# First block of a hedgehog attention kernel: x and the values' weights fetched first, a constant turned on TensorE until x is there, one tile's values and then the queries' folding in written order

## The chip, the cores and the metric

The kernel runs on one core of one Trainium2 chip. A core has five engines that run side by side, each taking its own instructions in order: TensorE (matrix products, PE in the profile), VectorE (DVE), ScalarE (ACT), GpSimd (POOL) and SyncE (SP), which here only issues DMA transfers. The metric is the device time of one execution in microseconds (us); the time of a kernel is the median over its runs.

## The reference

Two layers share their weights. Each layer adds an attention and a dense part to x, and each part reads x normalized over its 640 columns.

```python
qkv = (layernorm(x) @ wqkv)            # (2048, 640) @ (640, 1920): 32 heads of 20
pq = einsum("bhsd,hdf->bhsf", q, w_phi)   # a 20 x 20 matrix for each head; the same for k
phi_q = concat([softmax(pq), softmax(-pq)])           # 40 features a head; the same for k
kv, z = einsum(phi_k, v), sum(phi_k over s)
o = (phi_q @ kv) / (phi_q @ z + 1e-6)
x = x + o @ wo
x = x + mish(layernorm(x) @ w1 + b1) @ w2             # 640 -> 1536 -> 640
```

x is 2048 x 640, all in float32.

## The kernel before

**Tiles.** The 2048 rows are worked in 8 blocks of 256 rows, each of two tiles of 128. A block of x is normalized and then *turned*: TensorE transposes the rows in 128 x 128 pieces (ten for a block, `Transposed.step`, L280), so that the 640 columns lie on the partitions. Each float32 operand is split into a high part that TensorE takes at its faster type (made on ScalarE, tile names ending in `h`) and a low part, the difference (made on VectorE, names ending in `l`). A projection of one tile is then 30 products of 128 x 320: two halves, five row blocks, and three products each, high with high, high with low, low with high (`project_half`, L344).

**Folding.** The reference multiplies q and k by a small matrix per head after projecting. The kernel multiplies the weights instead: `fold_phi` (L227 to L243) makes, from the transposed raw weights and the block-diagonal `phi_bd`, the weights of the queries and, in a second call, of the keys. Each call has 30 products on TensorE: for each of five row blocks three in a first half and three in a second, the last with 40 columns only. For each half ScalarE takes the high part out of PSUM (L242) and VectorE the low part (L243).

**The first block.** Before any projection the kernel needs x's first block (fetch, statistics on VectorE at L250 and L252, a power on GpSimd at L259 and L260, and L262; the normalized rows on ScalarE; ten turnings and their two parts), the folded weights of the queries, and the values' weights (five pieces of 128 x 640, each fetched and split by `split`, L123). In attention's first block the order of work is v0, q0, v1, k0, q1, k1: values, queries and keys of tile 0 and 1. The keys' folding stands ahead of k0. Each piece of `features` (queries and keys) has steps on ScalarE, VectorE and GpSimd.

**What sets the order.** The whole kernel stands in one block whose order a planner makes for every engine: it takes the recorded instructions and places them by a simulated timeline. Inside `manual_schedule` the engines named keep the order in which the code is written. In the kernel before that is SyncE alone around the first block (L447), so the fetches stand in the order of the code, and the planner mixes the rest: the folding of the queries with x's turnings, with values and with the first queries. `act` (L110) also ties ScalarE's instructions that pass through it to their written order.

**Fetches.** Up to eight are under way; the ninth waits until the first has landed, and so on. The order at the start is: half of `phi_bd`, three raw pieces of the queries' weights, x's block 0, the other half of `phi_bd`, three more raw pieces, and, at their places in the plan, the head mask, x's block 1, b1, the five pieces of the values' weights (L126) and the keys' raw rows (L223). Folded weights are then written to DRAM for the second layer (`spill_qk_weights`, L190 and L191), and in block 1 `wo` is fetched and split, into tiles that the raw weights had (`make_five`, L141, L148, L149).

**Tiles in PSUM.** There are two `mm` tiles of two banks each and four `one` tiles of one bank. A fold of an even row block has an `mm`, of an odd one two `one`s.

Of the kernel before, what the change touches and what calls it, by code (L numbers as in the profile page):

```python
# [1 line left out]

# [39 lines left out]
def kernel(  # L42
# [40 lines left out]

    ident = const.tile([P, P], F32, name="ident")
    make_identity(nc, ident)
    b1s = const.tile([P, KF], F32, name="b1s")
    neg_half = const.tile([P, BT], F32, name="neg_half")
    nc.vector.memset(neg_half, -0.5)
# [16 lines left out]
    x1_d = dram.tile([S, D], F32, name="x1_d")  # L105
    x2_d = dram.tile([S, D], F32, name="x2_d")

    last_act = [None]

    def act(*args, **kw):  # L110

        if last_act[0] is None:
            ins = nc.scalar.activation(*args, **kw)
        else:
            with tc.issue_after(last_act[0]):
                ins = nc.scalar.activation(*args, **kw)  # L116
        last_act[0] = ins.ins
# [2 lines left out]
    def v_tile():  # L120
        return work.tile([P, VW], F32, tag="v", name="v", bufs=2)

    def split(hi, lo, src, stage):  # L123

        st = stage()[:, :D]
        nc.sync.dma_start(st, src)  # L126
        nc.scalar.activation(hi, st, AF.Copy)
        nc.vector.tensor_tensor(lo, st, hi.bitcast(F32), op=ALU.subtract)

# [31 lines left out]
    def r2_pair(j):  # L161
# [2 lines left out]
            return w[:, 0], w[:, 1]  # L164
        return tuple(wts.tile([P, D], F32R, tag=f"r2{s}{j}", name=f"r2{s}{j}") for s in "hl")

    def load_v_weights():

        ws = [r1_pair(k) for k in range(KD)]
        for k in range(KD):  # L170
            split(ws[k][0][:, D:2 * D], ws[k][1][:, D:2 * D], wv[k * P:(k + 1) * P, :],
                  (row_tile, row_tile, v_tile, v_tile, big_tile)[k])
        return ws

    def load_q_weights():
# [211 lines left out]
    def attend_first(layer, x_src, first):  # L387


        def fetch_normed(b):  # L390
            if layer:
                return load_turned(n2_d[b], [row_tile] * 3)
            xt = fetch(x_src, b)
            norm_scale(b, [norm_stats(t, xt) for t in range(BT)])
            return xt

# [32 lines left out]
                if b == NB - 1:  # L429
                    yield  # L430

        def values(xts, i, v):
            vv = v.rearrange("p (h d) -> p h d", d=DH + 1)
            act(vv[:, :, DH], ident[:, :H], AF.Copy, scale=0.0, bias=1.0)
            if i < BT:
                pv = project(xts, i, kv_ws, D, [one_tile(), one_tile()])
                for c in range(2):
                    act(vv[:, c * H // 2:(c + 1) * H // 2, :DH],
                        pv[c][:, :HC].rearrange("p (h d) -> p h d", d=DH), AF.Copy)
            else:  # L440
                pv = project(xts, i % BT, kv_ws, D)
                act(vv[:, :, :DH].rearrange("p (c h) d -> p c h d", c=2),
                    both(pv).rearrange("p c (h d) -> p c h d", d=DH), AF.Copy)
            yield

        if first is None:
            with tc.manual_schedule(engines={mybir.EngineType.SP}):  # L447
                bd = big_tile()[:120, :720].rearrange("p (t c) -> p t c", t=6)
                nc.sync.dma_start(bd[:, :3], phi_bd[:, :3])
                raw = load_raw(0, range(3))  # L450
                xt = fetch_normed(0)
                nc.sync.dma_start(bd[:, 3:], phi_bd[:, 3:])
                raw += load_raw(0, range(3, 6))
                nxt = normed(0, xt).all()
                q_ws = [r2_pair(k) for k in range(KD)]
                fold_phi(q_ws, bd, raw)
                kv_ws = load_v_weights()
                raw = load_raw(1)
            nc.sync.dma_start(mask, bass.AP(tensor=head_mask.tensor, offset=head_mask.offset,
                                            ap=[[1, 120], [120 * (DH + 1), 3]]))  # L460
        else:
            nxt, kv_ws = first
            q_ws = load_q_weights()
        for b in range(NB):
# [8 lines left out]
            vs = [v_tile() for _ in range(BT)]  # L473
            for n, (kind, t) in enumerate(order):
                t = int(t)
                i = b * BT + t
                if b == 0 and n == 1:
                    if layer:
                        load_k_weights(kv_ws)
                if b == 0 and n == 3:  # L480
                    if layer == 0:
                        fold_phi(kv_ws, bd, raw)
                    kva = one_tile()
                    nc.vector.memset(kva[:, :360], 0.0)
                if b == NB - 1 and n == 3:
# [12 lines left out]
                pending.append(g)  # L498
# [396 lines left out]
```

## Time and profile before

| | |
|---|---|
| median of 3 runs | 1383.88 us (1383.01 to 1385.57) |
| the profiled execution | 1385.02 us |
| its span, first to last instruction | 1383.2 us |
| TensorE busy | 1364.8 us, 99% |
| VectorE, ScalarE, GpSimd busy | 1082.0, 583.1, 440.5 us |
| granted TensorE clock by the page, mean | 0.999 |

The span lies 1.8 us below the time of the execution it belongs to. In the profile a row of the timeline has a start, a duration, the engine, the line of the kernel, the operation, the tile written and the tiles read, shapes, and a count where equal instructions follow each other; brackets give the time the engine stood before, and what ended it. Products overlap on TensorE, so the time of one is read from the starts of its neighbours and not from its own duration. A float32 product of the folding shows as two records; a turning and a projection's product are one each.

### The profile page before, as it was taken

What the parts mean: (1) busy time and instruction counts of PE and PEld (TensorE: products, weight loads), DVE (VectorE), ACT (ScalarE), POOL (GpSimd) and SP (SyncE); (2) the same over time, 40 slices, a digit from 0 to 9 for tenths busy, and PEclk for the clock granted to TensorE, in tenths of its full rate; (3) what the DMA queues carried; (4) which work ended last, traced back from release to release, by engine and by line L of the source; (5) the groups of instructions that cost most, each with busy time, mean ns of one, the idle gap of its engine ahead of it and who ended that gap; (6) DMA issues with size and microseconds to landing.
All of it is one profiled execution on the core that took longest, in us unless ns stands there. A gap on an engine that the chain in (4) does not pass through costs nothing. (4 is left out here: it accounts for less than half of the span.)

```text
span 1383.2 us, 30808 instructions
## 1 busy us (share of the span) xinstructions
PE 1364.8 (99%) x12866; PEld 1351.4 (98%) x12866; DVE 1082.0 (78%) x1820; ACT 583.1 (42%) x971; POOL 440.5 (32%) x334
## 2 busy tenths in 40 slices
PE   8999999999999999999999899999999999999998
PEld 7999999999999999999999899999999999999998
DVE  5799977886698887788769988988678776677775
ACT  4444434222445454545444333432235444444443
POOL 1353543353322222222234434453342111111112
PEclk9999999999999999999999999999999999999999
DMA  8532433779624432344474333458975211333200
GB/s 320 172 73 59 73 50 69 216 228 305 223 66 96 115 97 62 74 113 96 134 249 84 76 63 59 69 115 262 278 260 172 77 45 52 97 96 96 76 21 19
DMA packets 350276, 169.67 MB, mean 123 GB/s; under 512 B 287097, under 2 KB 323689, under 8 KB 350137
## 3 DMA queue, kind: packets, MB, share of 16 engines
q1 hardware_dynamic: 350137, 167.72, 45.0%
q8 instruction: 100, 1.64, 0.5%
q14 instruction: 39, 0.32, 0.1%
HBM read 104.76 MB, written 62.91 MB: 121 GB/s over the span
## 5 line engine op out<-in xcount | busy, mean ns | idle before, releaser
L733 PE MATMUL mm<-r2h,ol 128*128 128x320 f32 x1280 | 305.1, 309 | 0.8 <-ACT ol L716 0.8
L717 POOL TENSOR_TENSOR ol<-big,ol 128x512 fp32r<-128x512 f32 (+1 forms) x98 | 130.0, 1327 | 485.4 <-ACT ol L716 409.1
L691 PE MATMUL one<-xtl,r1h 128*128 128x256 f32 x960 | 268.2, 279 | 0.0
L691 PE MATMUL one<-xth,r1l 128*128 128x256 f32 x960 | 268.0, 279 | 0.0
L691 PE MATMUL one<-xth,r1h 128*128 128x256 f32 x960 | 265.9, 279 | 0.0
L733 PEld LDWEIGHTS mm<-r2h,ol 128*128 128x128 f32 x1280 | 219.1, 188 | 1.3 <-ACT ol L716 1.1
L733 PE MATMUL mm<-r2l,ol 128*128 128x320 f32 x640 | 197.3, 309 | 0.0
L344 PE MATMUL mm<-r1h,xtl 128*128 128x320 f32 x600 | 185.8, 310 | 1.7 <-DVE xtl L286 1.7
L344 PE MATMUL mm<-r1h,xth 128*128 128x320 f32 x600 | 187.4, 312 | 0.0
L344 PE MATMUL mm<-r1l,xth 128*128 128x320 f32 x600 | 186.0, 310 | 0.0
L691 PEld LDWEIGHTS one<-xtl,r1h 128*128 128x128 f32 x960 | 180.4, 188 | 0.0
L691 PEld LDWEIGHTS one<-xth,r1l 128*128 128x128 f32 x960 | 180.4, 188 | 0.0
L691 PEld LDWEIGHTS one<-xth,r1h 128*128 128x128 f32 x960 | 179.6, 188 | 0.0
L706 DVE TENSOR_SCALAR big<-big 128x512 f32<-128x512 f32 (+1 forms) x98 | 57.0, 582 | 109.9 <-ACT big L704 109.7
L379 POOL TENSOR_TENSOR r<-r,r 128x1280 f32<-128x1280 f32 x32 | 75.8, 2370 | 149.4 <-DVE r L378 143.5
L733 PEld LDWEIGHTS mm<-r2l,ol 128*128 128x128 f32 x640 | 120.2, 188 | 0.0
L708 ACT ACTIVATE big<-big,two 128x512 f32<-128x512 f32 (+1 forms) x98 | 70.2, 717 | 116.0 <-DVE big L707 116.0
L704 ACT ACTIVATE big<-one,b1s 128x256 f32<-128x256 f32 x192 | 80.9, 468 | 90.1 <-PE one L691 89.5
L716 ACT ACTIVATE ol<-big 128x512 fp32r<-128x512 f32 (+1 forms) x98 | 61.0, 622 | 136.3 <-DVE big L715 136.2
L344 PEld LDWEIGHTS mm<-r1h,xtl 128*128 128x128 f32 x600 | 112.7, 188 | 2.2 <-DVE xtl L286 2.1
L344 PEld LDWEIGHTS mm<-r1h,xth 128*128 128x128 f32 x600 | 112.7, 188 | 0.7
L344 PEld LDWEIGHTS mm<-r1l,xth 128*128 128x128 f32 x600 | 112.7, 188 | 0.1
(128 smaller groups left out, 3129.8 us busy)
## 6 DMA issues: line engine op xcount, KB each, us to landing
e_d<-r SPq DMA_DIRECT2D x128, 160.0 KB, 4.0
big<-e_d SPq DMA_DIRECT2D x32, 640.0 KB, 7.9
x_d<-xt SPq DMA_DIRECT2D x23, 640.0 KB, 3.7
xt<-x_d SPq DMA_DIRECT2D x22, 640.0 KB, 5.2
n_d<-xn SPq DMA_DIRECT2D x176, 80.0 KB, 2.2
xt<-in_x SPq DMA_DIRECT2D x16, 640.0 KB, 6.6
xn<-x_d SPq DMA_DIRECT2D x28, 320.0 KB, 4.7
v<-n_d SPq DMA_DIRECT2D x30, 256.0 KB, 3.1
```

The costliest lines, as they stand in the source:

```text
L344: nc.tensor.matmul(ps[:, :HC], a[:, sl], r, start=(k == 0 and n == 0), stop=(k == KD - 1 and n == 2))
L379: nc.gpsimd.tensor_tensor(eg, eg, r.unsqueeze(2).to_broadcast([P, 2 * H, DH]), op=ALU.mult)
L691: nc.tensor.matmul(ph[:, j, :], l, r, start=(n == 0), stop=(n == 3 * KD - 1))
L704: exps[0] = nc.scalar.activation(part(ta, 0)[:, j - js.start], ph[:, j, :], AF.Exp, bias=b1s[:, 2 * pr + j:2 * pr + j + 1]).ins
L706: nc.vector.tensor_scalar_min(e, e, E_CAP)
L708: nc.scalar.activation(r, n, AF.Ln, bias=two)
L716: nc.scalar.activation(ah[:, js], n, AF.Copy)
L717: nc.gpsimd.tensor_tensor(al[:, js], n, ah[:, js].bitcast(F32), op=ALU.subtract)
L733: nc.tensor.matmul(pys[t][:, c, :HC], l[:, j, sl], r, start=(f == 0 and n == 0), stop=(f == KF - 1 and n == 2))
```

## The change

Ahead of the planned block TensorE turns the constant `ident` 58 times into a PSUM tile that nobody reads. It begins when GpSimd has made the constant.

In the first block all five engines now keep the written order (`written`). It is: fetch x's block 0; fetch the five pieces of the values' weights; fetch `phi_bd` in one piece, the queries' raw rows, the keys' raw rows, and x's block 1 (`early`). Then the values' weights are split piece by piece with x's normalization and turnings in between; the second of the two normalized rows is made on VectorE (L480 in the changed kernel) in place of ScalarE. Then come the 30 products of tile 0's values, now with the row block as the outer loop and the two halves inside it, their copy out of PSUM, and the queries' folding. After that the planner has all engines again; the first piece of the loop (v0) is skipped there. Instructions inside `written` are not tied to each other by `act`.

```diff
+    warm = one_tile()
+    for _ in range(58):
+        nc.tensor.transpose(warm[:, :P], ident, ident)
...
+    @contextmanager
+    def written():
+        in_written[0] = True
+        with tc.manual_schedule(engines={getattr(mybir.EngineType, e) for e in (
+                "PE", "SP", "Activation", "DVE", "Pool")}):
+            yield
+        in_written[0] = False
...
-        if last_act[0] is None:
+        if last_act[0] is None or in_written[0]:
...
-    def split(hi, lo, src, stage):
-        st = stage()[:, :D]
-        nc.sync.dma_start(st, src)
+    def split(hi, lo, st):
         nc.scalar.activation(hi, st, AF.Copy)
         nc.vector.tensor_tensor(lo, st, hi.bitcast(F32), op=ALU.subtract)
...
+    def fetch_v(k):
+        st = (row_tile, row_tile, v_tile, v_tile, big_tile)[k]()[:, :D]
+        nc.sync.dma_start(st, wv[k * P:(k + 1) * P, :])
+        return st
...
-            xt = fetch(x_src, b)
+            xt = fetch(x_src, b) if b > 1 else early
...
         if first is None:
-            with tc.manual_schedule(engines={mybir.EngineType.SP}):
+            with written():
+                xt = fetch(x_src, 0)
+                mvs = [norm_stats(t, xt) for t in range(BT)]
+                kv_ws = [r1_pair(k) for k in range(KD)]
+                raws = [fetch_v(k) for k in range(KD)]
                 bd = big_tile()[:120, :720].rearrange("p (t c) -> p t c", t=6)
-                nc.sync.dma_start(bd[:, :3], phi_bd[:, :3])
-                raw = load_raw(0, range(3))
-                xt = fetch_normed(0)
-                nc.sync.dma_start(bd[:, 3:], phi_bd[:, 3:])
-                raw += load_raw(0, range(3, 6))
-                nxt = normed(0, xt).all()
+                nc.sync.dma_start(bd, phi_bd)
+                raw_q = load_raw(0)
+                raw = load_raw(1)
+                early = fetch(x_src, 1)
+                def make_v(k):
+                    split(kv_ws[k][0][:, D:2 * D], kv_ws[k][1][:, D:2 * D], raws[k])
+                make_v(0)
+                norm_scale(0, mvs)
+                xn = [row_tile() for _ in range(BT)]
+                act(xn[0], xt[:, 0, :], AF.Identity, bias=stats[:, 0, 1, 0:1], scale=stats[:, 0, 0, 0:1])
+                nc.vector.tensor_scalar(xn[1], xt[:, 1, :], stats[:, 0, 0, 1:2], stats[:, 0, 1, 1:2],
+                                        op0=ALU.mult, op1=ALU.add)
+                nxt = Transposed(xn)
+                for k in range(1, KD):
+                    make_v(k)
+                    if k < 4:
+                        nxt.step()
+                vs0 = [v_tile() for _ in range(BT)]
+                pv = [one_tile(), one_tile()]
+                for k in range(KD):
+                    for c in range(2):
+                        project_half(pv[c], nxt, 0, kv_ws, D, c, range(k, k + 1))
+                next(values(nxt, 0, vs0[0], pv))
                 q_ws = [r2_pair(k) for k in range(KD)]
-                fold_phi(q_ws, bd, raw)
-                kv_ws = load_v_weights()
-                raw = load_raw(1)
+                fold_phi(q_ws, bd, raw_q)
...
+            begun = b == 0 and not layer
+            vs = vs0 if begun else [v_tile() for _ in range(BT)]
...
+                if begun and n == 0:
+                    continue
```

More of the change, by code (lines that the diff above doesn't have):

```diff
@@ L1 @@
-from contextlib import ExitStack
+from contextlib import ExitStack, contextmanager
 import concourse.bass as bass
@@ L106 @@
     x2_d = dram.tile([S, D], F32, name="x2_d")
[L108 removed]
+    last_act, in_written = [None], [False]
+    @contextmanager
[5 more added lines that the diff above has]
+        in_written[0] = False
     def act(*args, **kw):
[L112 removed]
+        if last_act[0] is None or in_written[0]:
             ins = nc.scalar.activation(*args, **kw)
@@ L170, in load_v_weights @@
         for k in range(KD):
-            split(ws[k][0][:, D:2 * D], ws[k][1][:, D:2 * D], wv[k * P:(k + 1) * P, :],
-                  (row_tile, row_tile, v_tile, v_tile, big_tile)[k])
+            split(ws[k][0][:, D:2 * D], ws[k][1][:, D:2 * D], fetch_v(k))
         return ws
@@ L430, in queries, with values @@
                     yield
-        def values(xts, i, v):
+        def values(xts, i, v, pv=None):
             vv = v.rearrange("p (h d) -> p h d", d=DH + 1)
@@ L435, in values @@
             if i < BT:
-                pv = project(xts, i, kv_ws, D, [one_tile(), one_tile()])
+                pv = project(xts, i, kv_ws, D, [one_tile(), one_tile()]) if pv is None else pv
                 for c in range(2):
@@ L472, in attend_first @@
                 order = ("k0", "k1", "v0", "v1", "q0")
-            vs = [v_tile() for _ in range(BT)]
+            begun = b == 0 and not layer
+            vs = vs0 if begun else [v_tile() for _ in range(BT)]
             for n, (kind, t) in enumerate(order):
```

## The prediction

> **What bounds the kernel now.** I read the page first, then TensorE's row of the timeline for the first 60 us, then the rows of the other engines for the same stretch. The page says what the whole is bound by:
>
> ```profile
> PE 1364.8 (99%) x12866; PEld 1351.4 (98%) x12866; DVE 1082.0 (78%) x1820; ACT 583.1 (42%) x971; POOL 440.5 (32%) x334
> ```
>
> TensorE is busy for 99% of the 1383.2 us. A change in the first block can move the end only by what it adds to or takes from TensorE's lost time there: time in which it stands, and time in which it works slowly. The second is visible in TensorE's timeline (start, duration, count, and in brackets the idle time before):
>
> ```profile
> 4.23 3.30 PE L237 MATMUL mm<-big,raw 120*128 120x120 f32 x12 [4.23 <-DMA raw<-in_wqk_t]
> 9.88 2.03 PE L237 MATMUL mm<-big,raw 120*128 120x120 f32 x8 [2.35 <-DMA raw<-in_wqk_t]
> 11.84 1.07 PE L237 MATMUL mm<-big,r 40*128 40x40 f32 x4
> 13.15 0.90 PE L280 MATMUL one<-ident,xn 128*128 128x128 f32 x3 [0.23 <-ACT xn L113]
> ...
> 15.11 1.70 PE L280 MATMUL one<-ident,xn 128*128 128x128 f32 x7
> 16.61 1.47 PE L237 MATMUL mm<-big,raw 120*128 120x120 f32 x6
> ...
> 18.16 0.47 PE L344 MATMUL mm<-r2l,xth 128*128 128x320 f32 x1
> 18.43 1.57 PE L237 MATMUL one<-big,raw 120*128 120x120 f32 x10
> ...
> 36.57 0.83 PE L237 MATMUL mm<-big,raw 120*128 120x120 f32 x6
> 37.24 1.28 PE L237 MATMUL one<-big,raw 120*128 120x120 f32 x10
> ...
> 39.43 0.41 PE L237 MATMUL one<-big,r 40*128 40x40 f32 x2
> 39.77 0.70 PE L237 MATMUL mm<-big,raw 120*128 120x120 f32 x4
> 40.40 0.41 PE L237 MATMUL mm<-big,r 40*128 40x40 f32 x2
> ...
> 41.72 1.31 PE L280 MATMUL one<-ident,xn 128*128 128x128 f32 x10
> 42.87 0.83 PE L237 MATMUL mm<-big,raw 120*128 120x120 f32 x6
> 43.46 0.39 PE L344 MATMUL mm<-r1h,xth 128*128 128x320 f32 x1
> 43.69 0.31 PE L344 MATMUL mm<-r1l,xth 128*128 128x320 f32 x1
> ...
> 45.15 0.31 PE L344 MATMUL mm<-r1h,xtl 128*128 128x320 f32 x1
> ```
>
> Differences of starts give prices. A turning (transpose) costs 0.214 us early (seven from 15.11 to 16.61) and 0.115 late (ten from 41.72 to 42.87). A first-half fold of one row block (three products, six records) costs 0.67 late (36.57 to 37.24); a second half costs 0.97 (39.43 to 40.40). A projection product costs 0.146 late (ten steps from 43.69 to 45.15) and 0.27 early (18.16 to 18.43). So TensorE first runs at half rate. The rate rises inside the row at 18.43: ten at 0.214 would take 2.1 us and ten at 0.11 take 1.1, and it shows 1.57, so it rises about 0.6 us in, at 19.0. That is 5.85 us after the last gap, at 13.15.
>
> TensorE's loss at the start is therefore: standing 4.23 + 2.35 + 0.23 = 6.8 us; half rate for 3.3 us from 4.23, 3.0 us from 9.88 and 5.85 us from 13.15, together 12.2 us, half of it lost, 6.1 us. **Loss before: 12.9 us.** After that TensorE hardly waits.
>
> **The start after the change.** The constant is ready when GpSimd's select ends; x is the first fetch instead of the fifth. Rows of the timeline, the landing times of x's tile, and bytes by stretch (columns of the last two: length, then busy time of five engines, clock, DMA share, GB/s):
>
> ```profile
> 0.72 0.46 SPq L449 DMA_DIRECT2D big<-in_phi_bd  x1
> 0.99 0.29 POOL masks.py:199 TENSOR_SCALAR_AFFINE_SELECT ident<-ident 128x128 f32<-128x128 f32 x1
> 2.57 0.43 SPq L384 DMA_DIRECT2D xt<-in_x  x1
> 8.82 1.68 DVE L250 BATCH_NORM_STATS2 bn<-xt 128x6 f32<-128x320 f32 x4 [0.20 <-DMA xt<-in_x]
> ```
> ```profile
> DMA to landing us min/median/max: 3.8/6.7/7.7
> ```
> ```profile
> 2.00:4.00 2.00, 0.00 (x0) 0.00 (x0) 0.00 (x0) 0.00 (x0) 0.00 (x0) 1.00 0.90 289
> 4.00:6.00 2.00, 1.72 (x6) 1.47 (x7) 0.00 (x0) 0.00 (x0) 0.00 (x0) 1.00 1.01 358
> ```
>
> Issued at 0.72, x lands between 4.5 (the 3.8 of a fetch alone) and 7.0 (the 6.25 from 2.57 to 8.82, behind four others). Its 655 KB are through at 4.2 by the two stretches, so I take 5.2. From landing to the first turning the old chain took 13.15 - 8.82 = 4.33 us. VectorE's share of the new one (a split of 0.8 us ahead of the stats, which wait for GpSimd anyway; the second row of the pair made on VectorE beside ScalarE's) adds nothing. The rows are ready at 9.5 (8.8 to 11.3).
>
> The 58 turnings start at 1.3. When the rate rises is the open number. The nearest row is the 5.85 us above, so 7.2: 27 turnings at 0.214, 31 at 0.115, the last ends at 10.7. The ends: at full rate at once, 58 x 0.115 = 6.7, ending 8.0, and then x decides, 9.5; never, 58 x 0.214 = 12.4, ending 13.7. So x's turnings start at 10.7, and x would be ready 1.2 us earlier. [...]
>
> Ten turnings end at 11.85. The prices of what follows, on ScalarE and VectorE:
>
> ```profile
> 16.00 0.60 ACT L116 ACTIVATE xth<-one 128x512 fp32r<-128x512 f32 x1
> 31.33 0.71 ACT L116 ACTIVATE r<-mm 128x640 f32<-128x640 f32 x1 [2.79 <-PE mm L344]
> 31.94 1.73 ACT L116 ACTIVATE xn<-xt,stats 128x640 f32<-128x640 f32 x2
> 33.57 0.26 ACT L116 ACTIVATE v<-ident 128x32 f32<-128x32 f32 x1
> 34.01 0.73 ACT L148 ACTIVATE r2h<-raw 128x640 fp32r<-128x640 f32 x1
> 35.44 0.44 ACT L116 ACTIVATE v<-one 128x320 f32<-128x320 f32 x1 [0.70 <-PE one L344]
> 36.10 0.47 ACT L242 ACTIVATE r1h<-mm 128x360 fp32r<-128x360 f32 x1 [0.23 <-PE mm L237]
> ```
> ```profile
> 17.87 0.69 DVE L286 TENSOR_TENSOR xtl<-one,xth 128x512 fp32r<-128x512 f32 x1
> 20.87 0.82 DVE L128 TENSOR_TENSOR r1l<-big,r1h 128x640 fp32r<-128x640 f32 x1
> 23.71 1.67 DVE L250 BATCH_NORM_STATS2 bn<-xt 128x6 f32<-128x320 f32 x4 [0.43 <-DMA xt<-in_x]
> 37.27 0.53 DVE L243 TENSOR_TENSOR r1l<-one,r1h 128x360 fp32r<-128x360 f32 x1
> 41.45 0.45 DVE L243 TENSOR_TENSOR r1l<-mm,r1h 128x280 fp32r<-128x280 f32 x1
> ```
>
> The first high part takes 0.60 after four turnings (11.3 to 11.9), its low part 0.69 (12.55): TensorE loses 0.4 us. VectorE's rest (three splits and two low parts, 3.1 us) stays just ahead of the products. The 30 products end at 12.55 + 28 x 0.146 = 16.65. Work in it: 1.15 + 30 x 0.146 = 5.5. **Loss after: 11.1 us, a gain of 1.8** (2.9 if x decides).
>
> The fetches hold nothing up. Values' weights (five of 328 KB) follow x at 0.9 us each, the last by about 10, needed at 15. Phi's 346 KB and the queries' raw rows (1741 KB) are through by 2 + 4380/358 = 14.2, landed by about 15.7; the last is needed at 16.65 + 2.7 = 19.3. The keys' raw rows follow, through by 19.1 and needed from 30; block 1's x by 20.9, for stats on VectorE at about 24 whose result ScalarE takes at 36. The mask and b1, moved behind them, are used in the second half of the attention and in the dense layer.
>
> **Folding in one go, and what it does to the queues.** The work is the same. What changes is the order, which I read from the two built programs. Beyond block 1 they agree but for a few steps. After the 30 products, the changed TensorE order is: 24 fold products, 10 projections, 3 folds, 33 projections, 1 fold of k's second row block, the queries' last three folds, 14 projections, 2 folds that end k's second block, 3 folds, 3 projections, 12 folds, then block 1's turnings in between folds. ScalarE and VectorE hold this, in order:
>
> ```
> ScalarE: r1h_186<-one | r2h<-raw (wo) | r1h_190<-one | r<-mm | xn<-xt x2 |
>          v<-ident | v<-one x2 | r1h_184<-mm | ... xth<-one | r1h_184<-mm (2nd half)
> VectorE: ... xtl<-one | bn<-xt x4 | r1l_185<-mm (2nd half) | r1l_189<-mm
> ```
>
> ScalarE stops at r1h_186 until TensorE's 2 folds: 16.65 + 6.56 + 1.46 + 0.67 + 4.82 + 1.19 + 2.04 + 0.45 = 33.85, and 0.3 for three changes between fold and projection (43.46 to 43.69 took 0.23 in place of 0.146): 34.1. Behind it stand ready pieces, block 1's xn among them, that the old order had done before its fold (31.94). From there TensorE has 0.67 + 0.44 + 3.28 us of work and wants to turn block 1 at 38.6. ScalarE has 0.47 + 0.73 + 0.47 + 0.71 + 1.83 + 0.26 + 0.88 = 5.35, less about 0.1 overlap at eight seams (31.33 to 31.94 for an instruction of 0.71): 4.6 from 34.3, so 38.9. Its piece of wo is issued only when the queries' last folds end, at 31.3, and has to land first. In the same stretch before, these took:
>
> ```profile
> DMA to landing us min/median/max: 4.2/4.4/4.5
> ```
>
> That is 35.7, and ScalarE ends at 39.8. First wait: 0.3 to 1.2 us. Second, after four turnings (0.45): the next fold wants the first mm tile emptied, ScalarE 0.47 and VectorE 0.53 later, behind another VectorE step: 0.5 to 0.8. Third, the last block's first half wants that tile's second low part: on VectorE behind xtl (0.69) and four bn (1.67), then 0.45 itself. With xth at about 41.7 that is 44.5; TensorE is there after 0.97 + 0.45 + 0.97 + 0.22, at about 43.3: 1.2. **Together 2.0 to 3.2, taken 2.7**, and 0.3 for the changes of kind. All of it is cover lost: the old order had ScalarE level with TensorE there.
>
> Sum: -1.8 + 2.7 + 0.3 = **+1.2 us**, against the profiled 1385.02 us 1386.2. That run lies 1.1 us above the median 1383.88 (runs 1383.01 to 1385.57), so for a median I take 1385.1. The terms' ends (gain 1.0 to 2.9, waits 2.0 to 3.2) make -0.6 to +2.5 us, 1383.3 to 1386.4. A difference of 0.2%, 2.8 us, is about what a measurement of this kernel can tell from no change; the forecast is inside it.
>
> **Rivals.**
> *Turnings never raise the rate.* Then 58 end at 13.7, x's ten at 15.85, and products go at 0.27 until 5.85 us of them are through. Loss 13.7 + 1.1 + 2.9 + 0.4 = 18.1, 7.0 more than above: 1392.1, and 1390.6 with half that stretch. It decides once the 58 end later than 12.3 us, which is a half rate until 10.5. For it: the rate did not rise from 13.15 to 15.7, when five turnings stood among folds. Against: it rose after a stretch with seven turnings at its head, and turnings themselves ran at 0.115 when it was up. [...]
> *ScalarE's backlog stays hidden.* If tiles come free before TensorE asks, the 2.7 us are gone: -1.5, 1382.4, and 1381.3 with x deciding. For it: before, ScalarE was 42% busy. Against: the waits are in the order itself.
> *wo's piece comes late.* Eight spills of 328 KB are issued just before it; at 7 us landing (x's highest was 7.7) ScalarE ends 2.5 us later and TensorE with it: 1387.7. Against: those spills should be through by 32.
>
> **How the numbers follow.** The forecast 0.52, turnings that never raise the rate 0.20, backlog hidden 0.14, wo late 0.14. Slower by over 0.2%: 0.20, 0.13 of the late wo, 0.07 of the forecast's tail, 0.40. Faster: half of the hidden backlog and a little, 0.08. The rest, 0.52, is within 0.2%. For eight in ten the range goes from 1382.0, which holds most of the hidden backlog, to 1391.5, which holds the late wo and the quicker half of the first rival.
>
> **What would show it.** Right: the starts of the 58 turnings change from 0.214 to about 0.11 by 8 us, x's turnings begin at 9.6 to 11.2, the 30 products end near 16.7, and between 38 and 46 us TensorE stands three times, for ScalarE's v copy and twice for VectorE's r1l. Wrong: 0.214 up to the 58th; or no waits there; or a wait for wo on ScalarE above 2 us.

## The result, and the profile after

The changed kernel takes 1386.39 us (median of 22 runs, 1383.73 to 1389.19), the kernel before, run beside it, 1384.12 us (22 runs, 1381.83 to 1388.08). The ratio is 1.0016, with a 95% interval from 1.0009 to 1.0022: 2.2 us slower, 1.2 to 3.0, inside the range that was given and below the 0.2% taken as the bound of no change. Against the forecast of 1385.1 us it is 1.3 us more. The path to it is another one than the prediction's, and most of this part is about that.

The profiled execution took 1386.25 us, with a span of 1384.5 us, 1.3 us more than that of the kernel before. The page's first row has the same picture, TensorE at 99%, with 58 instructions more:

```profile
PE 1369.3 (99%) x12924; PEld 1355.6 (98%) x12924; DVE 1079.8 (78%) x1821; ACT 582.1 (42%) x970; POOL 440.0 (32%) x334
```

TensorE's timeline at the start (start, duration, count, idle time before with its releaser), and below it the stretches before and after 5.05 us for the turnings' line alone (length, busy time and count of TensorE's products and of its weight loads, granted clock, DMA share, GB/s):

```profile
1.34 8.34 PE L89 MATMUL one<-ident 128*128 128x128 f32 x58 [1.34 <-POOL ident masks.py:199]
9.52 1.26 PE L295 MATMUL one<-ident,xn 128*128 128x128 f32 x10
10.81 0.42 PE L359 MATMUL one<-r1h,xth 128*128 128x320 f32 x1
11.56 0.42 PE L359 MATMUL one<-r1h,xtl 128*128 128x320 f32 x1 [0.18 <-DVE xtl L301]
15.77 0.82 PE L252 MATMUL mm<-big,raw 120*128 120x120 f32 x6
```
```profile
1.34:5.05 3.71, 3.71 (x18) 3.71 (x19) 1.00 0.84 295
5.05:9.40 4.35, 4.35 (x41) 4.35 (x40) 1.00 0.97 321
```

18 turnings started in the first 3.71 us (0.21 us each) and 40 in the 4.47 us from 5.05 to 9.52 (0.11 each; the 41st that the row counts is one under way). So the rate rose under nothing but turnings, 3.7 us after they began; in the ten other profiles that have turnings at the start the step came 3.2 to 5.5 us after. The clock column reads 1.00 for both rows: before the trace's first clock record it shows full rate whatever the pitch. x's turnings follow without a gap, and the 30 products end at 15.77.

Then the three waits that were foreseen, on TensorE's timeline:

```profile
37.74 0.66 PE L295 MATMUL one<-ident,xn 128*128 128x128 f32 x4 [0.31 <-ACT v L129]
...
39.08 0.70 PE L252 MATMUL mm<-big,raw 120*128 120x120 f32 x4 [0.68 <-DVE r1l L258]
...
43.44 0.93 PE L252 MATMUL mm<-big,raw 120*128 120x120 f32 x6 [1.58 <-DVE r1l L258]
```

And one that was not, in block 1, with ScalarE's row behind it and three stretches around it (length, then busy time and count of TensorE, weight loads, VectorE, ScalarE, GpSimd, clock, DMA share, GB/s):

```profile
89.71 0.42 PE L359 MATMUL mm<-r1h,xth 128*128 128x320 f32 x1 [1.84 <-ACT r L129]
```
```profile
88.96 0.70 ACT L129 ACTIVATE r<-mm 128x640 f32<-128x640 f32 x1 [9.06 <-DMA e_d<-r]
```
```profile
83.60:87.00 3.40, 3.40 (x26) 3.40 (x25) 3.40 (x6) 0.00 (x0) 1.61 (x3) 1.00 0.91 141
87.00:90.40 3.40, 1.56 (x10) 1.30 (x10) 3.40 (x4) 1.44 (x2) 2.59 (x1) 1.00 0.34 63
90.40:93.80 3.40, 3.40 (x48) 3.07 (x50) 3.40 (x7) 1.42 (x4) 2.71 (x3) 0.50 0.00 0
```

ScalarE could not empty PSUM into the query's tile, because that tile's last content was still being written to DRAM. The kernel before has the same wait, but 4.3 us earlier, and TensorE does not stand for it:

```profile
84.68 0.71 ACT L116 ACTIVATE r<-mm 128x640 f32<-128x640 f32 x1 [3.28 <-DMA e_d<-r]
```

VectorE turns that content with one instruction, which the two plans place differently. Its row before and after:

```profile
76.69 1.50 DVE L424 STREAM_TRANSPOSE r<-r 128x1280 f32<-128x1280 f32 x1
```
```profile
80.88 1.50 DVE L439 STREAM_TRANSPOSE r<-r 128x1280 f32<-128x1280 f32 x1
```

So it comes 4.2 us later. VectorE's order is not all of it: GpSimd's product that makes this content ends at 73.96 us before and at 76.84 after, where two other instructions stand ahead of it on GpSimd:

```profile
71.59 2.37 POOL L379 TENSOR_TENSOR r<-r,r 128x1280 f32<-128x1280 f32 x1 [2.02 <-DVE r L378]
```
```profile
73.88 2.96 POOL L394 TENSOR_TENSOR r<-r,r 128x1280 f32<-128x1280 f32 x1
```

TensorE stands for 1.84 us, and a stretch of 3.4 us in which it was busy for 1.56 us is followed by one of the same length at half rate, which costs another 1.7 us, half of it.

Where the time went is read from the start of the k-th projection product, which is the same work in both kernels (us):

| product | before | after | difference |
|---|---|---|---|
| 30th | 26.29 | 15.62 | (other work lies ahead of it) |
| 210th | 62.39 | 62.65 | +0.26 |
| 401st | 94.83 | 98.14 | +3.31 |
| 1201st | 224.73 | 228.03 | +3.30 |
| TensorE's last instruction | 1378.78 | 1380.08 | +1.30 |

The 2 us that came back lie in later waits, above all one at 762 us, 2.75 us before and 1.64 us after (rows below).

### The profile page after: what moved, and what is told of

The parts are those of the page before. It is cut to its first block, busy times and chain, and to the rows that moved or that the text cites. A ratio compares the mean times of both kernels' runs of the same rounds, so it can differ in the third digit from the quotient of the medians.

```text
span 1384.5 us, 30920 instructions
## 1 busy us (share of the span) xinstructions
PE 1369.3 (99%) x12924; PEld 1355.6 (98%) x12924; DVE 1079.8 (78%) x1821; ACT 582.1 (42%) x970; POOL 440.0 (32%) x334
```

## The experiments

The theory after the first profiles: the start gained more than forecast, the three waits took it back, and the loss is the wait near 88 us with the half-rate stretch behind it. Rivals: the turnings are not what helps at the start; the loss is in the three waits; the loss is ScalarE waiting for wo's piece. The kernel before ran beside each set, at 1384.86, 1384.97 and 1384.33 us; kernels of different sets are best compared by their ratios to it. All kernels compute the whole of the reference.

**Without the turnings.**

```diff
-    warm = one_tile()
-    for _ in range(58):
-        nc.tensor.transpose(warm[:, :P], ident, ident)
```

> The changed kernel without its 58 turnings of the constant; all else as changed, though the order that the planner writes for block 1 on VectorE and GpSimd falls back to that of the kernel before. My theory: the turnings are what raises TensorE's rate (0.213 to 0.109 us a turning at 5.05 us in the changed kernel); without them x's turnings and the 30 products of tile 0's values (15.77 - 9.52 = 6.3 us at full rate there) run at half rate, and TensorE rises only after a stretch of unbroken work, between 13 and 19 us: first product at about 11.2, thirtieth product's end near 19 instead of 15.8, and 3 us (2 to 4.5) lost before 25 us. As block 1 has the other order, the 1.84 us wait at 87.9 and the half-rate stretch behind it (3.4 us at 0.5, so 1.7) should be gone. Sum against the changed kernel +3.0 - 3.3: 1386 us, 1384 to 1388. Rival (the turnings don't matter, x's wait decides): thirtieth product ends before 16.5, and the time is that of the changed kernel less the wait, 1383.

Measured: 1385.74 us, ratio 1.0007 (0.9998 to 1.0017). TensorE's timeline at its start:

```profile
9.54 2.39 PE L292 MATMUL one<-ident,xn 128*128 128x128 f32 x10 [9.54 <-ACT xn L123]
11.58 0.61 PE L356 MATMUL one<-r1h,xth 128*128 128x320 f32 x1
...
13.06 0.47 PE L356 MATMUL one<-r1h,xtl 128*128 128x320 f32 x1
13.33 0.47 PE L356 MATMUL one<-r1h,xth 128*128 128x320 f32 x1
```

x's turnings go at 0.2 us and products at 0.27, against 0.146 from 14.83 on: half rate. It rises at 14.7, after 5.1 us of work, and the thirtieth product starts at 17.32 in place of 15.62. The turnings are worth 1.7 us there, not the 3 I expected; x is ready at the same 9.5, so the rival that x decides is right for the start of x's turnings and wrong for their rate. There is no wait near 88 us. That this kernel is no slower than the changed one fits a loss in block 1 as large as the turnings' gain, and does not yet show it.

**The turnings alone**, put ahead of the kernel before (the lines above, added).

> The kernel before with the 58 turnings put ahead of its first block, nothing else changed. TensorE's queue is in order, so the first product of the fold cannot start before the last turning, near 8.3 us instead of 4.23; but all that follows runs at full rate instead of half until 19.05. My theory: the 5.9 us from 13.15 to 19.05 at half rate give back up to 2.9 us, less what x's turnings are late by, as their rows come behind the fold's evictions on ScalarE, which now start 4 us later (0 to 3 us): 1381 to 1385 us, and I take 1383.5. If the rows come 3 us late, 1385 or above and the turnings alone bring nothing: the gain at the start then hangs on x going first. Rival (the rate does not rise by turnings, or falls back in the waits): later than before by about 4 us, 1387 to 1388.

Measured: 1386.10 us, ratio 1.0007 (0.9998 to 1.0016): no gain. TensorE's timeline, and the three stretches around its wait:

```profile
16.65 0.90 PE L284 MATMUL one<-ident,xn 128*128 128x128 f32 x3 [2.69 <-ACT xn L117]
```
```profile
12.10:15.51 3.41, 1.86 (x12) 1.49 (x12) 2.17 (x8) 0.00 (x0) 1.09 (x3) 1.00 1.03 379
15.51:18.93 3.42, 2.28 (x11) 2.28 (x12) 3.09 (x11) 3.25 (x6) 0.39 (x2) 0.50 1.04 396
18.93:22.34 3.41, 3.41 (x18) 3.41 (x16) 3.27 (x8) 3.41 (x9) 1.75 (x2) 0.50 1.06 385
```

x's rows come 3.5 us later than in the kernel before (ScalarE makes the first from 15.68 us on, 12.17 before), TensorE stands for 2.69 us, and the rate that the turnings raised is lost again for 6.8 us. My 1383.5 was a miss; the case named for rows 3 us late came true, but not for the reason given. VectorE's rows show what held x:

```profile
11.44 0.97 DVE L247 TENSOR_TENSOR r2l<-mm,r2h 128x360 fp32r<-128x360 f32 x2 [10.56 <-ACT r2h L246]
12.33 1.67 DVE L254 BATCH_NORM_STATS2 bn<-xt 128x6 f32<-128x320 f32 x4
```

VectorE's order has the low parts of the first folds ahead of x's statistics. The folds start at 9.63 us behind the turnings, 4.23 before, and so the statistics start at 12.33, in the kernel before at 8.82, as x landed. Ahead of this order the turnings bring nothing.

**56 turnings in place of 58** (`range(56)`).

> The changed kernel with 56 turnings in place of 58: 0.2 us less of turnings, and the planner's order from block 1 on, on VectorE and GpSimd, is that of the kernel before (the order through the fold of the keys stays as changed). My theory: the wait of 1.84 us at 87.9 on the query tile's buffer comes from the changed order, and the half-rate stretch of 3.4 us behind it (1.7 us) from that wait. Both gone: the 401st product of a projection starts near 94.9 instead of 98.14 (94.83 in the kernel before), PEclk is 1.00 from 87 to 97, the three waits at 37.7, 39.1 and 43.4 stay (2.6 us together). Profiled run 1382.9, median 2 to 3 us below the changed kernel's, 1383.5 (1382.5 to 1384.5). Rival (the time lost at 88 us was slack that the end of the kernel does not see, the three waits alone make the difference): 401st product near 95, yet the time within 0.7 us of the changed kernel's, 1386.

Measured: 1386.26 us, ratio 1.0007 (0.9999 to 1.0016). The wait near 88 us is gone, and from the 210th to the 401st product it takes 31.94 us, against 35.49 in the changed kernel: that part of the theory holds, 3.5 us of it. The median is the changed kernel's all the same, so the theory about the median falls. The profile shows another loss, which the first profile of the changed kernel did not have. ScalarE's row, and TensorE's:

```profile
35.78 0.74 ACT L158 ACTIVATE r2h<-raw 128x640 fp32r<-128x640 f32 x1 [1.44 <-DMA raw<-in_wo]
```
```profile
37.52 0.93 PE L252 MATMUL mm<-big,raw 120*128 120x120 f32 x6 [1.12 <-ACT r L129]
```

ScalarE waits for wo's piece, and TensorE for ScalarE: from the 90th to the 210th product 30.67 us, 28.63 in the changed kernel's profile. This is the third rival of the prediction, in this execution.

**28 turnings**, the order on every engine being the changed kernel's (`range(28)`).

> The changed kernel with 28 turnings in place of 58; the order on every engine is the changed kernel's. The turnings then end at about 6.2 us and TensorE stands until x's rows are ready near 9.1 to 9.5 us. My theory: a stretch of 3.4 us in which TensorE is busy for less than half brings the rate down, as at 87 to 90.4 us of the changed kernel (1.56 of 3.40 us busy, 0.50 in the stretch after): x's turnings and the 30 products run at half rate for one or two such stretches, the rate rises again between 12 and 16 us, and the thirtieth product ends 2 to 3 us later than 15.77; 1388 us, 1386.5 to 1389.5. Rival 1 (a wait of 3 us does not lower the rate): 15.3 or 15.8 at the thirtieth product, 1386, within 0.5 of the changed kernel. Rival 2 (28 turnings are too few to raise the rate in the first place): as without turnings up to 25 us, thirtieth product near 19, 1389.

Measured: 1391.57 us, ratio 1.0048 (1.0035 to 1.0061). The three stretches from 3.11 us on:

```profile
3.11:6.53 3.42, 3.42 (x18) 3.42 (x18) 1.81 (x5) 0.74 (x1) 0.19 (x1) 1.00 1.00 366
6.53:9.94 3.41, 0.98 (x8) 0.74 (x8) 1.79 (x6) 1.35 (x2) 1.38 (x2) 1.00 1.04 338
9.94:13.35 3.41, 3.41 (x17) 3.41 (x16) 3.15 (x5) 3.16 (x7) 0.00 (x0) 0.50 1.04 332
```

A stand of 2.43 us, and the next stretch runs at half rate; both rivals are wrong. At the thirtieth product (16.57) it costs 1.0 us, less than expected. The whole, though, costs 5 us: in this profile a stretch at 44.1, two from 91.9 (the wait near 88 us is 3.29 us here) and one at 771.1 are at 0.5. Since the order is the changed kernel's, the wait near 88 us belongs to that order.

How it hangs on VectorE's turning of the query's tile is seen over all profiles. In six of them (the changed kernel twice, 28 turnings, and the runs below with wo's piece later at 58 turnings, SyncE alone, and the folding mixed) the turning starts 17.45, 18.20, 18.23, 18.35, 18.44 and 19.74 us after the 210th product, and TensorE stands for 1.04, 1.80, 1.84, 1.96, 2.03 and 3.29 us: each wait is the turning's time less 16.4 us, within 0.05. In six others, the kernel before among them, the turning starts 13.2 to 14.3 us after that product, and TensorE does not stand for this tile. So the lateness of the turning sets the wait one for one. The two runs with block 2's statistics later have yet another order, with their wait near 73 and 75 us.

**wo's piece later on ScalarE.** One of wo's five pieces is tied to ScalarE's written order, so that its split comes behind block 1's evictions; this holds for both layers.

```diff
-    def make_five(j, rows, low=nc.gpsimd):
+    def make_five(j, rows, low=nc.gpsimd, ordered=False):
...
-            make_parts(w, raws[k], low=low)
+            make_parts(w, raws[k], ordered=ordered and k == 1, low=low)
...
-        return list(make_five(KD, lambda k: wo[k * P:(k + 1) * P, :]))[1:]
+        return list(make_five(KD, lambda k: wo[k * P:(k + 1) * P, :], ordered=True))[1:]
```

> The changed kernel with one of the five pieces of wo, the one that ScalarE splits between the keys' fold's evictions (33.62 us in the changed kernel; 35.78 us in the run with 56 turnings, after 1.44 us of waiting for its transfer), put behind block 1's evictions in ScalarE's order. My theory: that piece is on the path. In the profiled run of the changed kernel it cost 0.7 us of ScalarE, which is the first of the three waits (0.31 at 37.74), and in other executions, where its transfer lands after 34 us, 1.1 to 2 us more and a stretch at half rate. Expected: the 91st product starts 0.3 to 0.6 us earlier than 44.13, the wait at 37.7 shrinks below 0.2, none on ScalarE for wo before 50 us. The order of block 1 on VectorE stays as changed, so the wait near 88 us stays (1 to 3 us), with its half-rate stretch. Time 0.5 to 1.5 us below the changed kernel's, 1385.3 (1384.3 to 1386.5). Rival (the piece is hidden; waits and half-rate stretches come from the r1l half behind VectorE's statistics alone): 91st product within 0.2 of 44.13, the time within 0.4 of the changed kernel's.

Measured: 1383.00 us, ratio 0.9990 (0.9981 to 0.9999), 3.4 us below the changed kernel's median (ratio 1.0016): more than twice what I expected. The first of the three waits is gone, the wait near 88 us is still there (1.04 us), in a stretch (87.71 to 91.12 us) in which TensorE was busy for 2.37 of 3.41 us, and the next one is at 1.00. The 91st product did not come earlier (44.91), since this execution got its rate 0.7 us later and lost it at 43.3. Part of the rest of the 3.4 us is seen at 762 us, in the second layer's first block, which the edit touches too. TensorE's rows of the kernel before, of the changed kernel and of this one:

```profile
764.72 0.83 PE L416 MATMUL one<-big,v 128*21 128x40 f32 x64 [2.75 <-POOL big L379]
```
```profile
766.42 0.83 PE L431 MATMUL one<-big,v 128*21 128x40 f32 x64 [1.64 <-POOL big L394]
```
```profile
764.64 0.83 PE L431 MATMUL one<-big,v 128*21 128x40 f32 x64 [1.02 <-POOL big L394]
```

In all ten profiles without the edit this wait is 1.52 to 2.75 us, and in five of them a stretch at half rate follows; in the four with it, 1.01 to 1.03 us, and none does.

**Block 2's statistics later**, with 56 turnings.

```diff
-            nc.vector.tensor_tensor(lo, ps[:, :n1 - n0], hi.bitcast(F32), op=ALU.subtract)
+            last_lo[0] = nc.vector.tensor_tensor(lo, ps[:, :n1 - n0], hi.bitcast(F32), op=ALU.subtract).ins
...
-            norm_scale(b, [norm_stats(t, xt) for t in range(BT)])
+            with tc.issue_after(last_lo[0]) if b == 2 else ExitStack():
+                mvs = [norm_stats(t, xt) for t in range(BT)]
+            norm_scale(b, mvs)
```

> The changed kernel with 56 turnings, and the statistics of block 2 (four readings of 128x320 on VectorE, 41.36 us in the changed kernel) put behind the last low part of the keys' fold. My theory: the third wait (1.58 at 43.44) is the low part r1l queued behind these four (1.67 us) and the low part of x's first two pieces; behind the fold they delay nobody, as block 2's rows are wanted only near 60 us. The third wait goes, the second grows to 1.2 at most, the 91st product starts 1 us earlier than in the run with 56 turnings less what that run lost to wo's late piece, near 43.5, and the windows between 36 and 48 us stay at full rate more often, so that of the executions fewer have a mean clock below 0.998. Time 1.0 to 2.5 us below the run with 56 turnings, 1384.5 (1383.5 to 1385.5). Rival (TensorE then waits for another thing as long, ScalarE's evictions being behind): the waits between 36 and 48 us sum to 2.5 us or more as before and the time stays within 0.5 of the run with 56 turnings.

Measured: 1384.89 us, ratio 1.0003 (0.9993 to 1.0013). The third wait is gone, as the theory has it, so the statistics were what it waited behind; but the 91st product is at 44.53, a microsecond later than expected, and a new wait stands further on, again for ScalarE's copy into the query's tile:

```profile
75.26 0.41 PE L361 MATMUL mm<-r1h,xth 128*128 128x320 f32 x1 [1.80 <-ACT r L129]
```

This profile also lost the rate once where TensorE did not stand at all, in the queries' folding:

```profile
18.99:22.40 3.41, 3.41 (x23) 2.79 (x21) 1.99 (x5) 1.43 (x4) 0.00 (x0) 1.00 1.04 341
22.40:25.81 3.41, 3.41 (x15) 3.41 (x14) 2.21 (x7) 0.40 (x1) 0.34 (x2) 0.50 1.03 397
```

By the medians it is 1.4 us below the run with 56 turnings, but that run is of another set and the intervals of the two ratios overlap: a gain in time is not shown.

**Both edits and 50 turnings.**

> Both edits together, and 50 turnings: they end near 8.8 to 9.6 us, as x's rows become ready. My theory (start gained, waits at 38 to 46 us mostly removed, no wait near 88 us since the planner's order of block 1 has the query tile's transposition early): first product 10.4, 91st product 42 to 42.8 (43.46 in the kernel before), 210th near 60.5 to 61 (62.39 before), 401st near 92.5 to 93.3 (94.83 before); so 1.5 to 2 us below the kernel before in the profiled run, and 0.5 to 2 us in the median, 1383 (1382 to 1384.5), ratio 0.9985 to 0.9995. Rival (each wait removed only lets the next resource be late: the planner's later order brings a new wait of 1.5 us or more before 110 us): 401st product at 94.8 or later, no gain on the kernel before.

Measured: 1383.42 us, ratio 0.9988 (0.9979 to 0.9997). The products are later than expected (91st 43.68, 210th 62.21, 401st 95.23): x was ready no earlier than with 58 turnings (first product 10.87), a stretch at half rate from 39.9 us took 1.7 us, and a wait of 0.95 us came at 72 us. The rival's mark, 94.8 at the 401st, was passed, but the kernel is still faster than before.

**SyncE alone in written order.**

```diff
-        with tc.manual_schedule(engines={getattr(mybir.EngineType, e) for e in (
-                "PE", "SP", "Activation", "DVE", "Pool")}):
+        with tc.manual_schedule(engines={mybir.EngineType.SP}):
...
-        if last_act[0] is None or in_written[0]:
+        if last_act[0] is None:
```

> The changed kernel with SyncE alone held to the written order in the first block; TensorE, ScalarE, VectorE and GpSimd are ordered by the planner. It tells what holding these four is worth. The planner again mixes fold products into tile 0's values and puts x's second rows and high parts elsewhere on ScalarE. My theory: little, since TensorE's work is the same and only its order differs: first product 1 to 2 us later than 10.81, but the fold already begun; the 90th product within 0.6 us of 34.02; block 1's order on GpSimd is as changed, so the wait near 88 us stays. Time within 0.8 us of the changed kernel's, 1386.4 (1385.3 to 1387.5). Rival (the written order is what makes the start fast, or what makes ScalarE's backlog): 90th product over 1 us later or earlier, and the time with it.

Measured: 1389.55 us, ratio 1.0032 (1.0020 to 1.0045). My theory was wrong: holding the other engines is worth 2 to 3 us (five runs). The first product starts at 13.77 in place of 10.81 and the thirtieth at 18.66. x's turnings wait 1.13 us for ScalarE, a fold product 0.61 us for its raw rows, and ScalarE later 3.41 us for wo's piece.

**The queries' folding mixed by the planner**, the rest in written order.

```diff
-                q_ws = [r2_pair(k) for k in range(KD)]
-                fold_phi(q_ws, bd, raw_q)
+            q_ws = [r2_pair(k) for k in range(KD)]
+            fold_phi(q_ws, bd, raw_q)
```

> The changed kernel with the queries' fold taken out of the written order: the planner mixes its products with tile 0's values and with later ones. My theory: holding the fold together is worth little either way, since the products are the same; the planner's mixing starts the fold a little earlier, fills the small gaps at 10.8 us, and keeps windows with products of 320 columns among those of 120, so none of 3.4 us at half rate in the fold as in the run with the statistics moved (22.4 us). Thirtieth projection product about 16.7 instead of 15.62, 90th 33.6 to 34.0, the wait near 88 us and the risk of wo's late piece as in the changed kernel: 1386 us, 1385 to 1387.5. Rival (the fold in one go is what makes wo's transfer start late, at 30.2 us instead of 25.4, and so ScalarE late): wo's issue comes at or before 28 us, ScalarE waits for it nowhere, the time is that of the run with wo moved, 1383 to 1384.

Measured: 1386.45 us, ratio 1.0017 (1.0008 to 1.0027), the changed kernel's time, with wo's transfer issued at 30.93 us. Folding in one go gives nothing and takes nothing, and is not what delays wo.

**wo's piece later in the kernel before** (the edit to `make_five`, nothing else).

> The kernel before with the same piece of wo put later on ScalarE, nothing else changed. It tells whether that edit is good for any kernel or only mends what the change made late. My theory: in the kernel before the piece's transfer is issued at 25.36 us and wanted at 34.01, so ScalarE does not wait for it, and TensorE has no wait over 0.2 us in 30 to 60 us: nothing to gain there; what is left is the small change of the planner's later order. Time within 0.7 us of the kernel before, ratio 0.9995 to 1.0005. Rival (the edit gives a gain of its own, at the second layer's start or by the later order): 1.5 to 2 us below the kernel before, ratio 0.9985 to 0.999, and the change itself then is worth nothing or a loss.

Measured: 1383.47 us, ratio 0.9992 (0.9983 to 1.0000). It is a small gain that the interval does not quite part from none, between what the theory and the rival said. In the row of the kernel before, at 34.01 us, ScalarE does not wait for this piece, so there was nothing to win there; but the wait at 762 us falls to 1.03 us, and all 11 runs have a mean granted clock of 0.999 or 1.000, while 11 of the 35 runs of the kernel before beside them have 0.998 or less.

**wo's piece later, 50 turnings.**

> The changed kernel with wo's piece later and 50 turnings; block 2's statistics stay where they are. With 50 the planner's order of block 1 on VectorE has the query tile's transposition early, as in the kernel before. Against the run with wo's piece alone it tells what the wait near 88 us is worth without the late wo, against the run with both edits what the statistics are worth. My theory: no wait over 0.6 us near 72 or 88 us; the third wait (1.8 us near 42) stays, with a half-rate stretch behind it in some executions; 210th product 61.6 to 62.4, 401st 93 to 94.5. Median 1382.7 (1381.8 to 1384). Rival (the wait near 88 us does no harm to the median once wo is mended): 1383.0 to 1383.5 as in the run with wo alone; or above 1384 if 50 turnings are too few to keep the rate until x is ready (a half-rate stretch begins between 8 and 12 us).

Measured: 1382.66 us, ratio 0.9986 (0.9977 to 0.9994): the median is as expected. No wait stands near 72 or 88 us, and the third wait is there (1.57 us). The places in the profile were a miss: the 210th product is at 65.43 us and the 401st at 97.42, 3 us later than expected, with two stretches at 0.50 ahead of them (from 22.4 and 46.3 us). This version beats the kernel before, and on the same chip lies 3.4 us below the changed kernel (next). The statistics' edit, which it leaves out, shows no gain. Against the kernel before with the same edit to wo it is 0.8 us faster by the medians, and the intervals of the two ratios overlap: whether the change has a gain of its own then stays open.

**The changed kernel again.**

> The changed kernel itself, beside these three on one chip, and a second profile of it. My theory: one execution's profile does not show what the median pays, since wo's piece lands before or after ScalarE wants it, from one execution to the next, and the grid of 3.41 us on which the rate is set lies otherwise in each. Expected: ScalarE waits 0 to 2.5 us for wo at 33.6 to 36 us; the wait near 88 us is there, 1 to 3.3 us; one to three stretches of 3.4 us at 0.5 somewhere in 36 to 48, 88 to 98 and 762 to 770 us; median 1385.5 to 1387, 1 to 2 us above the kernel before. Rival (the waits and the half-rate stretch at 90.4 us belonged to that one execution): no wait near 88 us and no stretch at 0.5 before 700 us.

Measured: 1386.05 us, ratio 1.0012 (1.0003 to 1.0021). The wait near 88 us is 1.80 us, with its stretch at 0.5, the 210th product starts at 62.64 and the 401st at 98.13, within 0.02 us of the first profile. ScalarE waited 0.26 us for wo's piece; the rival falls. At 762 us this execution paid what the first did not, after a wait of 1.98 us:

```profile
762.35:765.77 3.42, 1.44 (x73) 1.12 (x73) 3.42 (x3) 2.86 (x5) 2.75 (x1) 1.00 0.30 94
765.77:769.18 3.41, 3.41 (x72) 3.30 (x73) 3.41 (x5) 0.08 (x1) 0.69 (x1) 0.50 0.16 46
```

## Why the prediction was right, and where it was not

**Loss at the start: right in kind, 0.9 us off.** The gain was put at 1.8 us and measured 2.7: the 30 products ended at 15.77, not 16.65. This takes the sum's loss before, 12.9, as it stands. The term that was mis-sized is the time until the rate rises, taken as 5.85 us from one row of before; it was 3.7 here and 3.2 to 5.5 in the other profiles. x's turnings began at 9.52, so x and the last turning came together, near the case given as 2.9.

**Turnings that never raise the rate: wrong**, with a chance of 0.20. The pitch went from 0.21 to 0.11 us under nothing but turnings, 3.7 us after they began; in the run without them the rate rose after 5.1 us of other work.

**The three waits: right.** Forecast 2.0 to 3.2, taken 2.7, measured 0.31 + 0.68 + 1.58 = 2.57 us (0.67 + 0.67 + 1.23, the same sum, in the second profile), for ScalarE's v copy and twice for VectorE's r1l. The backlog that stays hidden (0.14) did not happen. Start and waits together leave 0.26 + 2.7 - 2.57 = 0.4 us at the 210th product for the changes of kind, put at 0.3.

**The step that failed** is the sentence "Beyond block 1 they agree but for a few steps", which counted block 1 itself at nothing. The few steps were VectorE's and GpSimd's: one instruction 4.2 us later made TensorE stand for 1.84 us, where before, at about the same place, it stood for 0.42, and for another thing (the row below is the kernel before's), and that wait cost 1.7 us more by the half rate behind it: +3.0 us from the 210th to the 401st product. Later waits gave 2.0 us back in that profile. So the profiled run (1386.2 forecast, 1386.25 measured) was right by luck, with errors on both sides: 0.9 of gain too little, and 3.0 - 2.0 = 1.0 of loss left out. The median was not: the forecast put it 1.1 us below the profiled run, as it lay before, and it lies 0.1 above. This goes with more executions that lose the rate once or more (16 of 22 runs of the changed kernel, and 7 of 11 later ones, with a mean granted clock of 0.998 or less; 11 of 35 of the kernel before). The wait near 88 us alone does not explain the median: with 56 turnings it was gone and the median was the same.

```profile
90.90 0.42 PE L344 MATMUL mm<-r1h,xtl 128*128 128x320 f32 x1 [0.42 <-DVE xtl L286]
```

**A second thing left out**: that a wait of 1.8 us cost 3.5 here (1.84 of standing, 1.7 by the half rate behind it). No term of the sum has it, and the runs of one kernel differ by it: of the changed kernel's 22, the three with a mean granted clock of 1.000 have a median of 1384.8 us, the four with 0.996 one of 1388.0. With the edit to wo, which shortens the wait at 762 us, the kernel before ran within 1382.05 to 1384.01 us.

**wo's piece late: it happens, but not always.** Before, its transfer was issued at 25.36 us and used at 34.01. After, it is issued at 30.2 (31.3 was forecast) and wanted at 33.6. ScalarE waited for it 0 and 0.26 us in two profiles of the changed kernel, 1.44, 2.57 and 3.41 us in those with 56 turnings, with none, and with SyncE alone, and 0, 0 and 0.16 us in those with 28 turnings, with the statistics later, and with the folding mixed. Moving the piece took 3.4 us off the changed kernel and 0.9 off the kernel before, and only with it did the ratio to the kernel before fall below 1. The edit also changes the planner's later order, so how much of the difference of 2.5 us is wo's landing and how much the order is not settled.

## What to carry to other kernels

Before an edit to the first block is costed, compare the plans of the following blocks on every engine, for each buffer with two copies: two turnings more or less moved a VectorE instruction, and the GpSimd one that feeds it, by microseconds 75 us later. A wait of TensorE can cost more than its length: the one of 1.84 us near 88 us cost 3.5 us, the one of 2.75 us at 762 us in the kernel before lost no rate. With that last wait down to 1.03 us, the 11 runs of the kernel before lay within 2.0 us, the 35 runs without the edit within 5.4 us. A second profile of the same kernel shows which waits are there each time and which come and go.

## What the runs showed of the hardware that was not expected

In the changed kernel's two profiles the changes of the granted clock lie whole multiples of 3.413 us apart: in the first it rises at 5.05, falls at 90.38 and rises at 93.79 us, 25 and 26 steps after the first, and in the second it falls at 89.93 and 765.77 us, 198 steps apart. The falls near 90 us lie 0.45 us apart in the two, while the 210th and 401st products start within 0.02 us of each other. The rate is down for one such step in the first profile (90.38 to 93.79 us) and for two with the turnings alone (15.51 to 22.34).

After the first rise, and outside the folding, stretches of one step were followed by one at 0.50 where TensorE was busy for 0.98 of 3.41 us (28 turnings, from 6.53 us), 1.44 of 3.42 (the changed kernel's second profile, from 762.35) and 1.56 of 3.40 (its first, from 87.00). They were not at 2.37 of 3.41 (wo's piece later, from 87.71), 2.39 of 3.42 (the same in the kernel before, from 758.59), and in the three below. In the kernel before TensorE stood for 2.75 us at 762 us and kept its rate, the wait lying in two stretches, 1.18 and 1.57 us of it:

```profile
759.73:763.15 3.42, 2.24 (x75) 1.91 (x73) 3.42 (x4) 1.30 (x2) 2.13 (x2) 1.00 0.63 141
763.15:766.56 3.41, 1.84 (x71) 1.78 (x72) 3.41 (x3) 1.69 (x4) 1.52 (x1) 1.00 0.11 34
766.56:769.97 3.41, 2.13 (x15) 1.87 (x14) 3.41 (x6) 0.00 (x0) 1.61 (x2) 1.00 0.05 16
```

The wait of 1.98 us in the changed kernel's second profile lay in one stretch whole, and the half rate behind it cost 1.7 us more, half of 3.41. Among the folding's products, stretches busy for 1.86 (the turnings alone, from 12.10), 1.89 (wo's piece later, from 39.92) and 2.31 of 3.41 us (SyncE alone, from 42.13) lost the rate, and those busy for 2.65 (SyncE alone, from 38.72) and 2.73 (wo's piece later, from 36.51) kept it. Two that the profile calls wholly busy lost it (18.99 to 22.40 us above, and 18.96 to 22.37 with wo's piece later and 50 turnings), and one in the changed kernel, as busy, kept it (18.70 to 22.11). The busy share alone does not part them, and what does is not shown.
